# Pairing the sums of the first key tiles and loading block 1's second features in stage one, in a two-layer attention and Mish kernel

## The chip, the cores and the metric

The kernel runs on one core of a Trainium2 chip. A core has a matrix engine (TensorE; PE in the profile, with its weight loads as PEld), a vector engine (VectorE, DVE), an engine for activation functions that also copies (ScalarE, ACT), a general engine (GpSimd, POOL), and a queue engine that issues transfers (SyncE, SP) to 16 DMA engines. Working memory is SBUF; matrix products land in PSUM, in banks. The metric is the device time of one execution in microseconds, and the median of several runs is compared.

## What is computed

A sequence of 2048 rows of 640 numbers goes through attention, dense, attention, dense, each on a layer-normed input and added to it. Attention has 32 heads of 20; its feature map is two softmaxes of a learned projection, one of it and one of its negative.

```python
pq = einsum("bhsd,hdf->bhsf", q, w_phi)          # and pk of k
phi = concatenate([softmax(p), softmax(-p)])     # 40 features for each head
kv = einsum("bhsf,bhsd->bhfd", phi_k, v);  z = phi_k.sum(rows)
o = einsum("bhqf,bhfd->bhqd", phi_q, kv) / (einsum("bhqf,bhf->bhq", phi_q, z) + 1e-6)
x = x + o @ wo
x = x + mish(norm(x) @ w1 + b1) @ w2
```

The key-value sum `kv` needs all rows before the first output row can be made. This splits attention into two stages.

## The kernel before

The 2048 rows are 16 tiles of 128, two to a block, 8 blocks. Products keep float32 precision by splitting both factors into a high and a low part and adding three products (15 matmuls for one half of a projection, 30 for both halves). In the profile the high and low parts of the normed, turned rows are `xth` and `xtl`; weights are `r1h`, `r1l` (keys and values) and `r2h`, `r2l` (queries).

**Stage one** (`attend_first`) runs over the blocks, and in a block over six steps, for instance k0, k1, v0, v1, q0, q1: a projection of keys, values or queries of tile 0 or 1 of the block. Each step is a Python generator. `keys` projects, makes the features in four further pieces (reduce, subtract, exponential, normalise) into a tile `e` of the tag `big` (five buffers) and at last adds the tile to the key-value sum `kva`: 32 small matmuls at L491, one for each head, recorded as 64. `values` evacuates the value rows with a column of ones into a tile `v` (two buffers). `queries` makes features likewise and stores them, transposed, in `e_d[b]` in DRAM with four stores a tile (L508). After each step `advance()` takes all pending generators one piece on, newest first, so the number of `yield`s in a generator sets how many steps later its matmuls come. In the first layer the rows of the next block are turned by TensorE transposes (L334, in `Transposed.turn`) in the last three steps of a block, by `nxt.step()`; in the second layer they come turned from DRAM, and GpSimd writes the low parts (L351). Within stage one the order on the engines is made at compile time by a scheduler that takes what it believes ready, earlier code first; it is not strictly the order of the code.

In block 7's fourth step, the features of block 0 (`load(0)`: two `big` tiles and a small one of the tag `ol`) and the first part of block 1's (`load_groups(1, 0)`, `load_end(1)`) are loaded, and the first two blocks of x are fetched.

**Stage two** (`attend_second`) has its order on TensorE and SP written out by hand. `finish_kv` copies and transposes the sum; `rest` is the last query tile (15), which fills waits; `average(b, t)` multiplies a tile's query features with the sum (L768) and divides. `load(b)` fetches a block's query features. The second part of block 1's features (`load_groups(1, 5)`, a `big` tile) is loaded here, between the two pieces of `finish_kv`, and `load(2)` after the averages of block 0. Query tiles 13 and 15 use the same buffer for their features.

The lines that matter here: L414 (projections), L491 (key-value sums), L334 (transposes), L351 (low parts), L503 (the transpose of query tile 13 on VectorE), L505 (those of the others), L508 (query stores), L720 and L725 (feature loads, large and small), L735 (transposes of the sum), L768 (averages), L135 (every ordered ScalarE copy).

Of the kernel before, what the change touches and what calls it, by code (L numbers as in the profile page):

```python
# [44 lines left out]
def kernel(  # L45
# [45 lines left out]
    for _ in range(30):  # L91
# [22 lines left out]
    x1_d = dram.tile([S, D], F32, name="x1_d")  # L114
    x2_d = dram.tile([S, D], F32, name="x2_d")

    last_act, in_written, last_low, last_load, last_recip, last_fold, last_product, last_sub = (
        [None], [False], [None], [None], [None], [None], [None], [None])

    @contextmanager  # L120
    def written():
# [7 lines left out]
    def act(*args, **kw):  # L129

        if last_act[0] is None or in_written[0]:
            ins = nc.scalar.activation(*args, **kw)
        else:
            with tc.issue_after(last_act[0]):
                ins = nc.scalar.activation(*args, **kw)  # L135
# [324 lines left out]
    def attend_first(layer, x_src, first):  # L460
# [8 lines left out]
            return xt  # L469

        pending = []

        def advance():
            for g in pending[::-1]:
# [5 lines left out]
        def keys(xts, i, v):  # L480
            e = big_tile()
            yield from features(project(xts, i % BT, kv_ws, 0, w=QC), e, False,
                                nc.vector if i == NT - 1 else nc.gpsimd)
            yield
            if i % BT == 0 and BT < i < NT - BT:
                yield
            for r in range(9):
                for j in range(4):
                    h = 3 * (4 * (r // 3) + j) + r % 3
                    if h < H:  # L490
                        nc.tensor.matmul(kva[32 * j:32 * j + DH + 1, 40 * r:40 * r + 40],  # L491
                                         v[:, (DH + 1) * h:(DH + 1) * (h + 1)], e[:, 40 * h:40 * h + 40],
                                         start=(i == 0 and r == 0), stop=(i == NT - 1), skip_group_check=True)

        def queries(xts, i, ps=None):
            e = query_tile(i)
            yield from features(project(xts, i % BT, q_ws, 0, w=QC) if ps is None else ps, e, True)

            b, t = divmod(i, BT)
            if i == NT - BT - 1:  # L500
                yield
                with tc.issue_after(last_recip[0]):
                    nc.vector.transpose(e, e)  # L503
            else:
                nc.vector.transpose(e, e)  # L505
            dst = e_d[b].rearrange("(j f) (t q s) -> t q f j s", f=32, t=BT, s=32)
            for q in range(4):
                nc.sync.dma_start(dst[t, q], e[32 * q:32 * q + 32].rearrange("f (j s) -> f j s", s=32))  # L508
                if b == NB - 1:
                    yield  # L510

        def values(xts, i, v):
            vv = v.rearrange("p (h d) -> p h d", d=DH + 1)
            act(vv[:, :, DH], ident[:, :H], AF.Copy, scale=0.0, bias=1.0)
            if i < BT:
                pv = project(xts, i, kv_ws, D, [one_tile(), one_tile()])
                for c in range(2):
                    act(vv[:, c * H // 2:(c + 1) * H // 2, :DH],
                        pv[c][:, :HC].rearrange("p (h d) -> p h d", d=DH), AF.Copy)
            else:  # L520
                pv = project(xts, i % BT, kv_ws, D)
                act(vv[:, :, :DH].rearrange("p (c h) d -> p c h d", c=2),
                    both(pv).rearrange("p c (h d) -> p c h d", d=DH), AF.Copy)
            yield

# [100 lines left out]
        for b in range(NB):  # L626
# [15 lines left out]
            for n, (kind, t) in enumerate(order):  # L642
# [63 lines left out]
                yield  # L706
                advance()

        return kva, o_ws, loaded, begun, xs, rest()

    def load(b):

        return load_groups(b, 0) + load_groups(b, 5) + load_end(b)

    def load_groups(b, g0):

        t = big_tile()
        src = e_d[b][120 * g0:120 * (g0 + 4) + P]
        src = bass.AP(tensor=src.tensor, offset=src.offset, ap=[[BLK, P], [120 * BLK, 5], [1, BLK]])
        nc.sync.dma_start(t.rearrange("f (g s) -> f g s", s=BLK), src)  # L720
        return [t[:, g * BLK:(g + 1) * BLK] for g in range(5)]

    def load_end(b):
        t = pair_tile(F32)
# [17 lines left out]
        yield  # L742

    def attend_second(x_src, x_dst, acc, fetches, makes, fetch_next, begin_next):
        kva, o_ws, loaded, begun, xs, rest = acc
        rows = {}
        div = [None]

# [57 lines left out]
        with tc.manual_schedule(engines={mybir.EngineType.PE, mybir.EngineType.SP}):  # L806
            kv = finish_kv(kva)
            next(rest)
            next(kv)
            loaded[1] = begun[0] + load_groups(1, 5) + begun[1]  # L810
            next(kv)
            next(rest)
            average(0, 0)
            average(0, 1)
            next(rest)
            loaded[2] = load(2)
            fetches[0]()
            average(1, 0)
            cur = Transposed(rows.pop(0)).all()
# [297 lines left out]
```

## Time and profile before

| | us |
|---|---|
| median of three runs (1356.41, 1356.49, 1360.51) | 1356.49 |
| the profiled execution | 1357.15 |
| its span | 1355.4 |
| stage one, first layer | about 36 to 246 |
| stage two, first layer | about 246 to 345 |
| dense, first layer | about 345 to 700 |
| stage one, second layer | about 700 to 907 |
| stage two, second layer | about 907 to 1006 |
| dense, second layer | about 1006 to 1355 |

How to read the rows that follow. A timeline row has its start and duration in us, the engine, the line, the operation, the output and the input, the shapes and a count of merged instructions; in square brackets stands the idle time before it and what ended it. A row of waits is: who waited, for whom, then the total in us, how often, and the longest. A group row gives count, total busy time, mean in ns, idle time before, and who ended most of it. Matmuls overlap in the pipeline, so their start times, and not their durations, tell what they cost. SPq is SP's queue: a row of it is the issue of a transfer, not the transfer.

### The profile page before, as it was taken

How to read it: one execution, taken by the hardware profiler on the slowest of the kernel's cores; microseconds unless marked ns; L12 is line 12 of the kernel's file. 1: busy time of each engine (PE TensorE's matmuls, PEld its weight loads, DVE VectorE, ACT ScalarE, POOL GpSimd, SP SyncE). 2: the span in 40 equal slices, each digit the busy share in tenths (PEclk: the TensorE clock that was granted, in tenths of full speed). 3: DMA queues.
4: the chain of work that ended last, by engine and by line, in shares of the span. 5: the costliest groups of instructions: out<-in, count | busy, mean ns of one | idle time of the engine just before them, and what ended most of it. 6: DMA issues, size and time to landing. Idle time of an engine off the chain costs nothing.

```text
span 1355.4 us, 30982 instructions
## 1 busy us (share of the span) xinstructions
PE 1347.9 (99%) x12896; PEld 1337.4 (99%) x12896; DVE 1061.2 (78%) x1799; ACT 575.7 (42%) x968; POOL 462.4 (34%) x417
## 2 busy tenths in 40 slices
PE   9999999999999999999999999999999999999999
PEld 9999999999999999999999999999999999999998
DVE  6888988886787887778769788788768776676775
ACT  5444444212454545445443334332236444444443
POOL 3355544334222222222225655634251211111112
PEclk9999999999999999999999999999999999999999
DMA  9544444698714442244474534548974221233200
GB/s 332 166 101 92 95 111 99 173 289 280 216 35 95 117 118 71 61 104 104 140 231 100 122 79 90 95 102 263 282 259 127 79 68 41 88 98 98 70 29 20
DMA packets 352629, 174.11 MB, mean 128 GB/s; under 512 B 287449, under 2 KB 324041, under 8 KB 352489
## 3 DMA queue, kind: packets, MB, share of 16 engines
q1 hardware_dynamic: 352489, 172.14, 46.9%
q8 instruction: 101, 1.65, 0.5%
q14 instruction: 39, 0.32, 0.1%
HBM read 106.23 MB, written 65.86 MB: 127 GB/s over the span
## 4 chain that ended last, share of the span: by engine, by line
PE 94%; DVE 2%; DMA 2%; POOL 1%; SPq 1%; ACT 0%; issue 0%; POOLq 0%; ACTq 0%
PE mm L414 26%; PE one L892 25%; PE mm L943 24%; PE one L414 12%; PE mm L768 2%; PE one L334 2%; PE one L491 1%; PE one L943 1%; DMA xt<-in_x 1%; PE one L768 1%; DVE r L448 1%; DMA raw<-in_wqk_t 0%; DVE m L439 0%; DMA v<-in_wv 0%; DVE r L442 0%; SPq L508 0%
## 5 line engine op out<-in xcount | busy, mean ns | idle before, releaser
L943 PE MATMUL mm<-r2h,ol 128*128 128x320 f32 x1240 | 296.1, 309 | 0.0
L918 POOL TENSOR_TENSOR ol<-big,ol 128x512 fp32r<-128x512 f32 (+1 forms) x98 | 131.1, 1338 | 477.7 <-ACT ol L917 419.5
L892 PE MATMUL one<-xtl,r1h 128*128 128x256 f32 x960 | 268.2, 279 | 0.0
L892 PE MATMUL one<-xth,r1l 128*128 128x256 f32 x960 | 268.0, 279 | 0.0
L892 PE MATMUL one<-xth,r1h 128*128 128x256 f32 x960 | 265.9, 279 | 0.0
L943 PEld LDWEIGHTS mm<-r2h,ol 128*128 128x128 f32 x1240 | 212.5, 188 | 0.0
L943 PE MATMUL mm<-r2l,ol 128*128 128x320 f32 x620 | 191.2, 309 | 0.0
L414 PE MATMUL mm<-r1h,xth 128*128 128x304 f32 (+1 forms) x600 | 185.2, 309 | 0.0
L414 PE MATMUL mm<-r1l,xth 128*128 128x304 f32 (+1 forms) x600 | 183.7, 306 | 0.0
L414 PE MATMUL mm<-r1h,xtl 128*128 128x304 f32 (+1 forms) x600 | 183.6, 306 | 0.2 <-POOL xtl L351 0.2
L892 PEld LDWEIGHTS one<-xtl,r1h 128*128 128x128 f32 x960 | 180.4, 188 | 0.0
L892 PEld LDWEIGHTS one<-xth,r1l 128*128 128x128 f32 x960 | 180.4, 188 | 0.0
L892 PEld LDWEIGHTS one<-xth,r1h 128*128 128x128 f32 x960 | 179.6, 188 | 0.0
L907 DVE TENSOR_SCALAR big<-big 128x512 f32<-128x512 f32 (+1 forms) x98 | 57.2, 583 | 110.0 <-ACT big L905 109.8
L909 ACT ACTIVATE big<-big,two 128x512 f32<-128x512 f32 (+1 forms) x98 | 70.1, 715 | 116.1 <-DVE big L908 116.1
L917 ACT ACTIVATE ol<-big 128x512 fp32r<-128x512 f32 (+1 forms) x98 | 60.9, 622 | 137.6 <-DVE big L916 137.4
L905 ACT ACTIVATE big<-one,b1s 128x256 f32<-128x256 f32 x192 | 80.9, 468 | 89.0 <-PE one L892 88.5
L450 POOL TENSOR_TENSOR r<-r,r 128x1280 f32<-128x1280 f32 x32 | 77.2, 2413 | 118.9 <-DVE r L449 100.8
L943 PEld LDWEIGHTS mm<-r2l,ol 128*128 128x128 f32 x620 | 116.4, 188 | 0.0
L414 PEld LDWEIGHTS mm<-r1h,xth 128*128 128x128 f32 x600 | 112.8, 188 | 0.9
L414 PEld LDWEIGHTS mm<-r1h,xtl 128*128 128x128 f32 x600 | 112.8, 188 | 0.4 <-POOL xtl L351 0.4
L414 PEld LDWEIGHTS mm<-r1l,xth 128*128 128x128 f32 x600 | 112.8, 188 | 0.1
(161 smaller groups left out, 3142.7 us busy)
## 6 DMA issues: line engine op xcount, KB each, us to landing
e_d<-r SPq DMA_DIRECT2D x128, 160.0 KB, 4.2
big<-e_d SPq DMA_DIRECT2D x32, 640.0 KB, 8.0
x_d<-xt SPq DMA_DIRECT2D x23, 640.0 KB, 4.8
xt<-x_d SPq DMA_DIRECT2D x22, 640.0 KB, 5.3
n_d<-xn SPq DMA_DIRECT2D x168, 80.0 KB, 2.3
xt<-in_x SPq DMA_DIRECT2D x16, 640.0 KB, 4.4
xn<-x_d SPq DMA_DIRECT2D x28, 320.0 KB, 4.4
v<-n_d SPq DMA_DIRECT2D x30, 256.0 KB, 3.0
```

What stands on the lines that cost most here:

```text
L334: nc.tensor.transpose(ps[:, c, t * P:(t + 1) * P], self.rows[t][:, (c0 + c) * P:(c0 + c + 1) * P], ident)
L414: last_product[0] = nc.tensor.matmul(ps[:, :w], a[:, sl], r, start=(k == 0 and n == 0), stop=(k == KD - 1 and n == 2)).ins
L448: nc.vector.tensor_reduce(r, eg, axis=AX.X, op=ALU.add)
L450: ins = scale.tensor_tensor(eg, eg, r.unsqueeze(2).to_broadcast([P, 2 * H, DH]), op=ALU.mult).ins
L768: nc.tensor.matmul(po[c][64 * q:64 * q + 64, GW * j:GW * j + w], phs[g][:n, s0:s0 + 64], kvb[:n, g, :w], start=True, stop=True)
L892: nc.tensor.matmul(ph[:, j, :], l, r, start=(n == 0), stop=(n == 3 * KD - 1))
L905: exps[0] = nc.scalar.activation(part(ta, 0)[:, j - js.start], ph[:, j, :], AF.Exp, bias=b1s[:, 2 * pr + j:2 * pr + j + 1]).ins
L907: nc.vector.tensor_scalar_min(e, e, E_CAP)
L909: nc.scalar.activation(r, n, AF.Ln, bias=two)
L917: nc.scalar.activation(ah[:, js], n, AF.Copy)
L918: nc.gpsimd.tensor_tensor(al[:, js], n, ah[:, js].bitcast(F32), op=ALU.subtract)
L943: ins = nc.tensor.matmul(pys[t][c][:, :HC], (ah, ah, al)[n][:, j, t * P:(t + 1) * P], w, start=(f == 0 and n == 0), stop=(f == KF - 1 and ...
```

## The change

- `held(i)` sets how many steps the key-value sum of tile i is held: in the first layer 2 and 0 for block 0, 3 and 1 for block 1, 3 and 2 for blocks 2 to 5, 1 and 0 for block 6, none for block 7; in the second layer 1 and 0 for all blocks but the last. Before it was 1 and 0 for blocks 2 to 6 in both layers, and 0 for blocks 0, 1 and 7. Two tiles of a block so come in the same step, the newer first, and the first group to come opens the accumulation.
- `v_halves`: in even blocks of the first layer the value tiles are two half tiles of the tag `ol` (six buffers, otherwise unused then) in place of `v`; the ones and the values are then written half by half.
- In block 7's fourth step all of block 1's features are loaded: the first part as before, the rest by `load_rest(1)` into three `ol` tiles with four DMAs. `load_groups(1, 5)` in stage two and the separate small load go.
- `load(2)` comes ahead of the second piece of `finish_kv`, and on SP behind the last query store issued so far (`last_store`).

```diff
+        def held(i):
+            b, t = divmod(i, BT)
+            if layer or b == NB - 2:
+                return int(t == 0 and b < NB - 1)
+            return {0: (2, 0), 1: (3, 1), NB - 1: (0, 0)}.get(b, (3, 2))[t]
...
-            if i % BT == 0 and BT < i < NT - BT:
+            for _ in range(held(i)):
                 yield
+            opens = not summed[0]
+            summed[0] = True
...
-                                         v[:, (DH + 1) * h:(DH + 1) * (h + 1)], e[:, 40 * h:40 * h + 40],
-                                         start=(i == 0 and r == 0), stop=(i == NT - 1), skip_group_check=True)
+                                         v[1][c][:, (DH + 1) * g:(DH + 1) * (g + 1)], e[:, 40 * h:40 * h + 40],
+                                         start=(opens and r == 0), stop=(i == NT - 1), skip_group_check=True)
...
+    def v_halves(apart):
+        if apart:
+            return None, [pair_tile(F32).rearrange("p a s -> p (a s)")[:, :VW // 2] for _ in range(2)]
+        v = v_tile()
+        return v, [v[:, :VW // 2], v[:, VW // 2:]]
...
-            vs = [v_tile() for _ in range(BT)]
+            vs = [v_halves(not layer and b % 2 == 0) for _ in range(BT)]
...
-                    begun = load_groups(1, 0), load_end(1)
+                    loaded[1] = load_groups(1, 0) + load_rest(1)
...
+    def load_rest(b):
+        out = []
+        for g0 in (5, 7, 9):
+            t = pair_tile(F32)
+            n = min(2, 10 - g0)
+            src = e_d[b][120 * g0:120 * (g0 + n - 1) + P]
+            src = bass.AP(tensor=src.tensor, offset=src.offset, ap=[[BLK, P], [120 * BLK, n], [1, BLK]])
+            nc.sync.dma_start(t[:, :n], src)
+            out += [t[:, 0], t[:, 1]]
+        nc.sync.dma_start(t[:80, 1], e_d[b][1200:])
+        return out
...
             next(rest)
+            with tc.issue_after(last_store[0]):
+                loaded[2] = load(2)
             next(kv)
-            loaded[1] = begun[0] + load_groups(1, 5) + begun[1]
             next(kv)
             next(rest)
             average(0, 0)
             average(0, 1)
             next(rest)
-            loaded[2] = load(2)
             fetches[0]()
```

The values' evacuation, for a tile held in halves:

```diff
+            for w in [v[0]] if v[0] is not None else v[1]:
+                ones = w.rearrange("p (h d) -> p h d", d=DH + 1)[:, :, DH]
+                act(ones, ident[:, :ones.shape[1]], AF.Copy, scale=0.0, bias=1.0)
+            if v[0] is None or i < BT:
                 for c in range(2):
-                    act(vv[:, c * H // 2:(c + 1) * H // 2, :DH],
+                    act(v[1][c].rearrange("p (h d) -> p h d", d=DH + 1)[:, :, :DH],
                         pv[c][:, :HC].rearrange("p (h d) -> p h d", d=DH), AF.Copy)
```

More of the change, by code (lines that the diff above doesn't have):

```diff
@@ L471, in attend_first @@
         pending = []
+        summed = [False]
+        def held(i):
[3 more added lines that the diff above has]
+            return {0: (2, 0), 1: (3, 1), NB - 1: (0, 0)}.get(b, (3, 2))[t]
         def advance():
@@ L512, in values @@
         def values(xts, i, v):
[L513 to L516, printed above, removed]
+            for w in [v[0]] if v[0] is not None else v[1]:
+                ones = w.rearrange("p (h d) -> p h d", d=DH + 1)[:, :, DH]
+                act(ones, ident[:, :ones.shape[1]], AF.Copy, scale=0.0, bias=1.0)
+            pv = project(xts, i % BT, kv_ws, D, [one_tile(), one_tile()] if i < BT else None)
+            if v[0] is None or i < BT:
                 for c in range(2):
-                    act(vv[:, c * H // 2:(c + 1) * H // 2, :DH],
+                    act(v[1][c].rearrange("p (h d) -> p h d", d=DH + 1)[:, :, :DH],
                         pv[c][:, :HC].rearrange("p (h d) -> p h d", d=DH), AF.Copy)
             else:
-                pv = project(xts, i % BT, kv_ws, D)
-                act(vv[:, :, :DH].rearrange("p (c h) d -> p c h d", c=2),
+                act(v[0].rearrange("p (c h d) -> p c h d", c=2, d=DH + 1)[:, :, :, :DH],
                     both(pv).rearrange("p c (h d) -> p c h d", d=DH), AF.Copy)
@@ L707, in rest @@
                 advance()
-        return kva, o_ws, loaded, begun, xs, rest()
+        return kva, o_ws, loaded, xs, rest()
     def load(b):
@@ L744, in attend_second @@
     def attend_second(x_src, x_dst, acc, fetches, makes, fetch_next, begin_next):
-        kva, o_ws, loaded, begun, xs, rest = acc
+        kva, o_ws, loaded, xs, rest = acc
         rows = {}
```

8 lines of the change are left out of this document (5 added, 3 removed).

## The prediction

> **What bounds the kernel now.** I read the page first, then TensorE's waits, then the chain of waits, then the timeline of TensorE around every key-value sum (L491) and around the two places where it stands idle.
>
> ```profile
> span 1355.4 us, 30982 instructions
> PE   1347.9 (99%) x12896; PEld 1337.4 (99%) x12896; DVE 1061.2 (78%) x1799; ACT 575.7 (42%) x968; POOL 462.4 (34%) x417
> ```
> ```profile
> PE 94%; DVE 2%; DMA 2%; POOL 1%; SPq 1%; ACT 0%; issue 0%; POOLq 0%; ACTq 0%
> ```
> ```profile
> PE one L334 <- ACT r L135: 1.8, 2, 1.3
> ```
> ```profile
> PEld one L491 <- issue: 3.4, 19, 0.2
> ```
>
> TensorE is the bound (94% of the chain) and is fed nearly always. The change multiplies the same matrices in the same shapes, so it can win only three things: the 1.8 us in which the transposes of L334 wait for ScalarE, twice (once per layer); the cost of entering and leaving a sum, which shows as 0.18 us (3.4 / 19) of weight-load idle at each group; and waits on late operands. It can lose only by new waits.
>
> The execution profiled took 1357.15 us, its span of 1355.4 and 1.75 around it; the median of the three runs shown is 1356.49. I work out a difference in the profiled execution and take it off the median. 0.3% (4.07 us) is about what a measurement of this kernel can tell from no change.
>
> **Part 1: what a pair saves.** A single sum between projections, a pair, a single ahead of four transposes, and four transposes alone, each from the last matmul before it to the second after it (the first one after starts slow):
>
> ```profile
> 78.55 0.30 PE L414 MATMUL mm<-r1h,xtl 128*128 128x304 f32 x1
> 78.78 0.83 PE L491 MATMUL one<-big,v 128*21 128x40 f32 x64
> ...
> 79.79 0.30 PE L414 MATMUL mm<-r1l,xth 128*128 128x304 f32 x1
> 79.93 0.30 PE L414 MATMUL mm<-r1h,xtl 128*128 128x304 f32 x1
> ```
> ```profile
> 110.93 0.30 PE L414 MATMUL mm<-r1h,xtl 128*128 128x304 f32 x1
> 111.17 1.48 PE L491 MATMUL one<-big,v 128*21 128x40 f32 x128
> ...
> 112.81 0.30 PE L414 MATMUL mm<-r1l,xth 128*128 128x304 f32 x1
> ```
> ```profile
> 62.22 0.30 PE L414 MATMUL mm<-r1h,xtl 128*128 128x304 f32 x1
> 62.45 0.83 PE L491 MATMUL one<-big,v 128*21 128x40 f32 x64
> 63.21 0.65 PE L334 MATMUL one<-ident,xn 128*128 128x128 f32 x4
> ...
> 63.85 0.31 PE L414 MATMUL mm<-r1l,xth 128*128 128x320 f32 x1
> ```
> ```profile
> 92.83 0.31 PE L414 MATMUL mm<-r1h,xtl 128*128 128x320 f32 x1
> 92.98 0.60 PE L334 MATMUL one<-ident,xn 128*128 128x128 f32 x4
> ...
> 93.56 0.31 PE L414 MATMUL mm<-r1l,xth 128*128 128x320 f32 x1
> ```
>
> Matmuls start 0.14 us apart (79.79 to 79.93), so two steps, 0.28 to 0.29 us, come off each stretch. A single costs 1.24 - 0.28 = 0.96 us, a pair 1.88 - 0.28 = 1.60: **one pair instead of two singles saves 0.32 us.** A single with transposes behind it costs 1.63 - 0.28 = 1.35, the transposes alone 0.73 - 0.29 = 0.44: the single is 0.91 there, so **standing ahead of transposes saves 0.05.**
>
> The Trainium skill (TensorEngine Tiling (Array Packing), Key Properties) says that a change of the tiling mode drains TensorE; the sums use 32-column tiles and the transposes the whole array, so by it the neighbourhood saves no drain, and the trace agrees with its 0.05 us. If instead a neighbour saved a whole entry and exit (0.32 us), the six pairs moved there would give 1.9 us, not 0.3.
>
> First layer, tiles 0 to 3: now 2 x 0.91 + 2 x 0.96 (tiles 0 and 1 already stand ahead of transposes) = 3.74; after, two pairs ahead of transposes, 2 x 1.55 = 3.10; saves 0.64. Blocks 2 to 5 are pairs already and move two steps on, to transposes: 4 x 0.05 = 0.2. Second layer: four singles become two pairs, 0.64. Together 1.5 us of pure TensorE time.
>
> **Part 2: what a later sum uncovers.** The singles of tile 2 stand, in both layers, ahead of (or inside) the first projection of block 2 and cover the wait for its operand; the change moves them behind it. With the 0.32 of the first pair, TensorE comes to that operand 0.96 + 0.32 = 1.28 us sooner. In the first layer (VectorE writes the operand, TensorE uses it):
>
> ```profile
> 81.68 0.41 DVE L351 TENSOR_TENSOR xtl<-one,xth 128x256 fp32r<-128x256 f32 x1
> ```
> ```profile
> 81.05 0.30 PE L414 MATMUL mm<-r1l,xth 128*128 128x304 f32 x1
> 81.19 0.30 PE L414 MATMUL mm<-r1h,xth 128*128 128x304 f32 x1
> ...
> 82.73 0.44 PE L414 MATMUL mm<-r1h,xtl 128*128 128x304 f32 x2
> ```
>
> It is ready at 82.09 and used at 82.73: 0.64 us of slack, and the compiler's schedule has already put the second half's matmuls (from 81.19) ahead of the ones that need it. Bounds for this layer's 0.64: all of it, if the schedule fills again, or nothing, if 1.28 - 0.64 = 0.64 is waited. I take 0.6, as this very place shows the filling. In the second layer GpSimd writes it and is late already:
>
> ```profile
> 746.72 0.74 POOL L351 TENSOR_TENSOR xtl<-xn,xth 128x256 fp32r<-128x256 f32 x1
> ```
> ```profile
> 744.36 0.83 PE L491 MATMUL one<-big,v 128*21 128x40 f32 x64
> ...
> 747.05 0.30 PE L414 MATMUL mm<-r1l,xth 128*128 128x304 f32 x1
> 747.51 0.41 PE L414 MATMUL mm<-r1h,xtl 128*128 128x304 f32 x1 [0.15 <-POOL xtl L351]
> ...
> 749.94 0.83 PE L491 MATMUL one<-big,v 128*21 128x40 f32 x64
> ```
>
> Here the step from 747.05 to 747.51 holds 0.32 us of waiting. If the order of the matmuls stays as it is, TensorE still goes on at 747.5 whatever was saved before, and behind it stands a pair (1.60) instead of the single at 749.94 (0.96): a **loss of 0.64**. If the schedule fills the wait with the other half or the pair, it gains 0.64 + 0.32 = 0.96. The rows show filling once (81.19) and none once (747.05); I take a gain of 0.3 and keep -0.96 and +0.64 as ends.
>
> **Part 3: the start of stage two.** First layer:
>
> ```profile
> 243.30 1.50 DVE L503 STREAM_TRANSPOSE r<-r 128x1280 f32<-128x1280 f32 x1
> ```
> ```profile
> 236.05 3.34 SPq L508 DMA_DIRECT2D e_d<-r  x4
> 245.27 0.38 SPq L720 DMA_DIRECT2D big<-e_d  x1
> 245.75 7.23 SPq L508 DMA_DIRECT2D e_d<-r  x4
> ```
> ```profile
> 243.31 0.16 POOL L430 MEMSET r<- 128x32 f32 x1 [1.28 <-DMA e_d<-r]
> ```
> ```profile
> 255.44 0.74 ACT L135 ACTIVATE r<-one 128x304 f32<-128x304 f32 x2 [5.16 <-DMA e_d<-r]
> ```
> ```profile
> 255.92 0.44 PE L334 MATMUL one<-ident,xn 128*128 128x128 f32 x2 [1.28 <-ACT r L135]
> ```
>
> Query tile 13 is transposed by 244.80, but its four stores stand on SP behind block 1's second features (L720 at 245.27, which waits for the last sums to free its buffer) and share the DMA engines with it: 7.23 us to issue against 3.34 for tile 12's. They land at 255.4; only then may ScalarE write tile 15 into the same buffer, free its two PSUM banks, and let the transposes go on: 1.28 us idle. The change takes that load out (block 1's rest comes in stage one, in three small tiles and four DMAs for the former two) and puts load(2) behind the stores by issue_after. Tile 12's stores took 243.3 - 236.05 = 7.2 us from first issue to last landing; from 244.85 that is 252.1, when TensorE still has work to 254.6 (255.92 - 1.28). So the **1.28 us goes.** What is late next is the split of these rows for the first projection of stage two; ScalarE and VectorE do it right behind the transposes, so it comes 1.28 sooner too. The second layer's wait has the same cause:
>
> ```profile
> 916.49 0.44 PE L334 MATMUL one<-ident,xn 128*128 128x128 f32 x2 [0.53 <-ACT r L135]
> ```
>
> 0.53 goes with it: **1.81 us in all**. Bounds: 0, if the stores stay late, and 1.81; I take 1.8, the room being 254.6 - 252.1 = 2.5 us. load(2), three DMAs, now waits on SP for the last sums too, but behind the stores; behind it wait only the first weight fetch and load(3), and its data are used by block 2's averages, after the whole projection of block 0. Its two big buffers are those of the last key tiles, so load(3) takes load(0)'s, no later than now. The four DMAs of stage one stand where SP already waits for sums.
>
> **ScalarE.** Even blocks of the first layer evacuate their values into two half tiles:
>
> ```profile
> L135 ACT ACTIVATE v<-mm 128x640 f32<-128x640 f32 x28 | 19.8, 707 | 50.1 <-PE mm L414 50.1
> L135 ACT ACTIVATE v<-ident 128x32 f32<-128x32 f32 x32 | 8.2, 258 | 0.0
> L135 ACT ACTIVATE v<-one 128x320 f32<-128x320 f32 x8 | 3.3, 434 | 5.2 <-PE one L414 5.2
> ```
>
> 2 x 0.434 - 0.707 = 0.16, and 0.26 for a second column of ones: 0.42 us for each of six tiles, 0.26 for the two of block 0, 3.0 us in all, hidden by the idle that the first row has ahead of it (50.1 us over 28). Its price without cover is those 3.0 us.
>
> **Sum:** 1.8 + 0.6 + 0.2 + 0.3 = 2.9 us off. 1357.15 becomes 1354.25 in a profiled execution, and **1353.6** against the median.
>
> **Rivals.** *All of it arrives*: 1.81 + 0.64 + 0.2 + 0.96 = 3.6, 1352.9. For it: the scheduler filled at 81.19. Against it: at 747.05 it did not see GpSimd late. *Only the boundary pays*, because the later sums uncover the waits of part 2, or because the schedule slips the sums apart again (as at 78.78, inside a projection): 1.8 + 0 + 0.2 - 0.64 = 1.4, 1355.1. *Slower: SP is blocked in stage one.* Its small tiles are the ones that now hold block 6's values, free only when tiles 12 and 13 are summed:
>
> ```profile
> SPq L720 <- PE one L491: 9.7, 2, 8.3
> ```
>
> Today SP waits up to 8.3 us there with nothing urgent behind. If the four new loads are put ahead of four query stores, these are 8.3 us late, ScalarE cannot evacuate the next query tile, and TensorE, with one projection (4.2 us, 30 x 0.14) of spare bank, loses 4.1 us a layer; from 4.2 us of lateness on it costs. Both layers: 8.2 - 2.9 = 5.3 slower, 1361.8; one: 1357.7. Against it: a load is placed only when its tile is free.
>
> **From this to the numbers.** Forecast 0.50, all of it 0.20, only the boundary 0.18, slower 0.12. The first three lie within 0.3% (1352.4 to 1360.6); a sum of 3.6 comes over 4.07 only with half a microsecond of scatter (1357.15 against 1356.49), for which I give 0.13 out of these three. Of the slower case, 0.08 is over 0.3%. Same 0.79. The range is from the full gain with that scatter, 1352.1, to one blocked layer, 1357.7.
>
> **What would show it.** TensorE's waits of L334 on ScalarE gone; the L491 groups, ten in a layer, become eight pairs, each near 1.48 us, and the weight loads' idle there near 16 x 0.18 = 2.9; the stores of tile 13 issued within 3.5 us of 244.9; the wait for GpSimd near 747 tells layer two's sign. Wrong would be: idle of L414 on L351 of over 1 us, stores of tile 13 still behind a load, or SP waits on L491 with L508 behind them.

## The result and the profile after

The changed kernel takes 1359.85 us (median of 19 runs, 1356.89 to 1365.95), the kernel before beside it 1356.83 (19 runs, 1355.73 to 1360.96): a ratio of 1.0019, 95% interval [1.001, 1.0028]. It is slower by 0.2%, where 0.2% less was forecast. The execution profiled took 1358.03 us, with a span of 1356.3, 0.9 over the span before. The page of the changed kernel (L421, L509, L341, L358, L326, L456 and L457 are the former L414, L491, L334, L351, L319, L449 and L450) and its waits of TensorE:

```profile
span 1356.3 us, 31003 instructions
...
PE 81%; DVE 8%; POOL 1%; DMA 1%; issue 0%; SPq 0%; ACT 0%; DVEq 0%; POOLq 0%; ACTq 0%
```
```profile
PE mm L421 <- DVE xtl L358: 2.3, 3, 1.1
PE one L509 <- POOL big L457: 1.2, 1, 1.2
PE mm L421 <- POOL xtl L358: 0.4, 1, 0.4
```

VectorE now holds 8% of the chain, where it held 2%. The two waits of L334 on ScalarE are gone from the list, and new ones stand in it: three for VectorE's third low part (xtl, 128x256) and, in the second layer, one of a sum for GpSimd (1.2 us); the projection's wait for GpSimd's low part was there before and has grown from 0.2 to 0.4 us. Where they fall is seen by comparing a fixed event of each stage, the third transposes made for the next block, in TensorE's timeline of the kernel before and then of the changed one:

```profile
102.45 0.38 PE L334 MATMUL one<-ident,xn 128*128 128x128 f32 x2
...
130.75 0.38 PE L334 MATMUL one<-ident,xn 128*128 128x128 f32 x2
...
159.04 0.38 PE L334 MATMUL one<-ident,xn 128*128 128x128 f32 x2
...
187.32 0.38 PE L334 MATMUL one<-ident,xn 128*128 128x128 f32 x2
```
```profile
102.11 0.38 PE L341 MATMUL one<-ident,xn 128*128 128x128 f32 x2
...
109.26 0.41 PE L421 MATMUL mm<-r1h,xtl 128*128 128x304 f32 x1 [0.61 <-DVE xtl L358]
...
131.22 0.38 PE L341 MATMUL one<-ident,xn 128*128 128x128 f32 x2
...
138.82 0.41 PE L421 MATMUL mm<-r1h,xtl 128*128 128x304 f32 x1 [1.07 <-DVE xtl L358]
...
160.78 0.38 PE L341 MATMUL one<-ident,xn 128*128 128x128 f32 x2
...
167.95 0.41 PE L421 MATMUL mm<-r1h,xtl 128*128 128x304 f32 x1 [0.64 <-DVE xtl L358]
...
189.91 0.38 PE L341 MATMUL one<-ident,xn 128*128 128x128 f32 x2
```

At 102 the changed kernel is 0.34 us ahead; one block later it is 0.47 behind, then 1.74, then 2.59. Each of the three steps between the rows has one wait, at the first projection of blocks 3, 4 and 5, and is longer by that wait and 0.2 us more. Stage one of layer one loses 2.93 us there (87.80 against 84.87).

Stage two wins. Its beginning in the first layer, in TensorE's timeline before and then after (the transposes of the sums, the ten transposes of the averages, the first averages behind them):

```profile
246.72 0.49 PE L735 MATMUL one<-ident,xn 128*120 128x128 f32 x3
...
253.55 1.09 PE L334 MATMUL one<-ident,xn 128*128 128x128 f32 x8
...
256.29 1.38 PE L768 MATMUL mm<-kvb,big 120*64 120x63 f32 x40
```
```profile
249.23 0.49 PE L767 MATMUL one<-ident,xn 128*120 128x128 f32 x3
...
256.05 1.31 PE L341 MATMUL one<-ident,xn 128*128 128x128 f32 x10
257.29 0.80 PE L800 MATMUL mm<-kvb,big 120*64 120x63 f32 x20
```

From the first row to the last it was 9.57 us and is 8.06. The ten transposes stand in one group with no idle; from their start to the averages it is 1.24 us where it was 2.74, of which 1.28 was the wait. To the start of the dense part the whole stage gains 1.52 us, in the second layer 1.07. Stage one of the second layer, from its first key projection to the transposes of the sums, goes from 207.75 us (699.97 to 907.72) to 208.82 (700.98 to 909.80). Together: 0.23 from a later start (stage one's first transposes at 36.23 against 36.00), -0.57 up to the rows at 102, +2.93, -1.52, +1.07, -1.07, and -0.07 in what is left is 1.0 us at the last matmul, about the 0.9 of the spans.

**Why the low part is late.** VectorE and GpSimd of the kernel before, ahead of block 4's first projection (VectorE's rows first):

```profile
133.34 0.68 DVE L351 TENSOR_TENSOR xtl<-one,xth 128x512 fp32r<-128x512 f32 x1
...
135.39 0.41 DVE L351 TENSOR_TENSOR xtl<-one,xth 128x256 fp32r<-128x256 f32 x1
135.72 0.54 DVE L449 RECIPROCAL r<-r 128x64 f32<-128x64 f32 x1
136.18 0.16 DVE L319 SCALAR_TENSOR_TENSOR stats<-mv,stats 128x1 f32<-128x1 f32 x2
```
```profile
136.34 2.97 POOL L450 TENSOR_TENSOR big<-big,r 128x1280 f32<-128x1280 f32 x1 [0.24 <-DVE stats L319]
```

And of the changed kernel:

```profile
133.63 0.68 DVE L358 TENSOR_TENSOR xtl<-one,xth 128x512 fp32r<-128x512 f32 x1
134.23 0.54 DVE L456 RECIPROCAL r<-r 128x64 f32<-128x64 f32 x1
134.69 1.48 DVE L446 TENSOR_REDUCE m<-r 128x32 f32<-128x640 f32 x2
136.09 2.34 DVE L326 SCALAR_TENSOR_TENSOR stats<-mv,stats 128x1 f32<-128x1 f32 x2
138.35 0.41 DVE L358 TENSOR_TENSOR xtl<-one,xth 128x256 fp32r<-128x256 f32 x1
```
```profile
132.32 2.37 POOL L457 TENSOR_TENSOR big<-big,r 128x1280 f32<-128x1280 f32 x1
134.78 0.46 POOL L323 TENSOR_SCALAR ve<-mv 128x1 f32<-128x1 f32 x2
135.33 0.70 POOL L324 TENSOR_TENSOR stats<-ve,neg_half 128x2 f32<-128x2 f32 x1
135.99 2.36 POOL L457 TENSOR_TENSOR big<-big,r 128x1280 f32<-128x1280 f32 x1
```

The second low part (128x512) starts at nearly the same time in both (133.34 and 133.63), and the third, whose high part ScalarE had written by 133.13, starts 3 us later, at 138.35 against 135.39. Two things make this up. The reciprocal and the next block's layer norm statistics now stand ahead of it; and the statistics, which took 0.16 us, take 2.34, as long as GpSimd's multiplication runs beside them. The edit moved the sums on TensorE, but the order of VectorE and GpSimd is made by the same scheduler at compile time, and here it has turned round. At block 3 the statistics stood ahead of the low part in the kernel before too, but early (0.17 us at 102.92); now they come at 105.04, behind one multiplication of GpSimd, and take 2.38 us beside the next.

### The profile page after: what moved, and what is told of

Read it like the earlier page. It is cut to its first block, busy times and chain, and to the rows that moved or that the text cites. A ratio compares the mean times of both kernels' runs of the same rounds, so it can differ in the third digit from the quotient of the medians.

```text
span 1356.3 us, 31003 instructions
## 1 busy us (share of the span) xinstructions
PE 1346.3 (99%) x12896; PEld 1336.2 (99%) x12896; DVE 1066.0 (79%) x1799; ACT 577.3 (43%) x982; POOL 462.7 (34%) x417
## 4 chain that ended last, share of the span: by engine, by line
PE 81%; DVE 8%; POOL 1%; DMA 1%; issue 0%; SPq 0%; ACT 0%; DVEq 0%; POOLq 0%; ACTq 0%
PE one L924 25%; PE mm L975 24%; PE mm L421 17%; PE one L421 10%; PE mm L800 2%; DVE r L455 2%; DVE m L446 1%; PE one L341 1%; PE one L509 1%; DVE r L523 1%; DVE xn L813 1%; PE one L975 1%; DVE r L449 1%; DVE xtl L358 1%; DMA e_d<-r 1%; DVE r L456 0%
## 5 line engine op out<-in xcount | busy, mean ns | idle before, releaser
L421 PE MATMUL mm<-r1h,xtl 128*128 128x304 f32 (+1 forms) x600 | 183.7, 307 | 2.7 <-DVE xtl L358 2.3
L421 PE MATMUL mm<-r1h,xth 128*128 128x304 f32 (+1 forms) x600 | 184.7, 308 | 0.0
L421 PE MATMUL mm<-r1l,xth 128*128 128x304 f32 (+1 forms) x600 | 183.6, 306 | 0.0
L457 POOL TENSOR_TENSOR r<-r,r 128x1280 f32<-128x1280 f32 x32 | 78.6, 2458 | 113.1 <-DVE r L456 104.3
L421 PEld LDWEIGHTS mm<-r1h,xtl 128*128 128x128 f32 x600 | 112.8, 188 | 3.6 <-DVE xtl L358 3.1
L421 PEld LDWEIGHTS mm<-r1h,xth 128*128 128x128 f32 x600 | 112.8, 188 | 0.5
L421 PEld LDWEIGHTS mm<-r1l,xth 128*128 128x128 f32 x600 | 112.8, 188 | 0.1
```

The source lines that it names most:

```text
L421: last_product[0] = nc.tensor.matmul(ps[:, :w], a[:, sl], r, start=(k == 0 and n == 0), stop=(k == KD - 1 and n == 2)).ins
L457: ins = scale.tensor_tensor(eg, eg, r.unsqueeze(2).to_broadcast([P, 2 * H, DH]), op=ALU.mult).ins
```

## The experiments

The table gives for each kernel the three steps between third transposes (as in the rows above; 28.3 before), stage one of the second layer, and the median against the kernel before that ran beside it.

| kernel | three steps of stage one, layer one | stage one, layer two | median | ratio [95%] |
|---|---|---|---|---|
| before | 28.30, 28.29, 28.28 | 207.75 | 1356.83 | |
| changed | 29.11, 29.56, 29.13 | 208.82 | 1359.85 | 1.0019 [1.001, 1.0028] |
| e0_again | 32.40, 28.45, 29.91 | 210.45 | 1360.27 | 1.0025 [1.0016, 1.0035] |
| e1_held_back | 29.68, 28.28, 28.29 | 208.96 | 1358.40 | 1.0006 [0.9997, 1.0015] |
| e2_boundary | 28.30, 28.29, 28.28 | 207.77 | 1354.56 | 0.9981 [0.9972, 0.999] |
| e5_stats_behind | 28.23, 28.22, 28.23 | 208.91 | 1356.11 | 0.9996 [0.9986, 1.0005] |
| e6_best | 28.27, 28.29, 28.28 | 207.68 | 1353.48 | 0.9969 [0.9958, 0.998] |
| e7_moved_alone | 28.25, 33.67, 28.23 | 208.12 | 1360.37 | 1.0019 [1.001, 1.0028] |
| e9_layer2_first | 31.77, 28.32, 29.81 | 208.22 | 1359.88 | 1.0018 [1.001, 1.0027] |
| e10_layer2_later | 28.28, 28.28, 28.28 | 210.66 | 1355.71 | 0.9989 [0.9981, 0.9997] |
| e11_memset_behind | 28.28, 28.28, 28.28 | 207.18 | 1353.32 | 0.997 [0.9958, 0.9982] |
| e12_layer2_whole | 28.28, 28.29, 28.28 | 207.78 | 1354.38 | 0.9983 [0.9973, 0.9992] |

**e0_again**: the changed kernel, unedited.

> The changed kernel once more, for a second profile of it. Theory (VectorE's order): in stage one of layer one each first projection of blocks 3, 4 and 5 waits for the third low part (xtl of 128x256), because the two small statistics instructions stand ahead of it on VectorE and last about as long as GpSimd's multiplication of the second key tile (2.36 us). The first profile had 0.61, 1.07 and 0.64 us of it and lost 2.85 us between the third transposes of block 2's stage and those of block 5's. This run shows the same three waits, 2 to 4 us in all; the median time is 2.5 to 3.5 us over the kernel before. Rival (chance of one execution): the waits stand at other places, or the loss between these two points is under 1 us.

The waits are there, but not the same three. The profile of this execution lists

```profile
PE mm L421 <- DVE xtl L358: 3.8, 2, 2.4
```

and the first of them, with VectorE's statistics of x and low part ahead of it, and the granted clock (the number behind the count in brackets) in stretches of 1 us behind it:

```profile
98.34 1.28 DVE L314 BATCH_NORM_STATS2 bn<-xt 128x6 f32<-128x320 f32 x3 [4.02 <-DMA xt<-in_x]
...
110.09 0.41 DVE L358 TENSOR_TENSOR xtl<-one,xth 128x256 fp32r<-128x256 f32 x1
```
```profile
111.00:112.00 1.00, 1.00 (x6) 0.53 0.78 305
112.00:113.00 1.00, 1.00 (x6) 0.50 0.07 23
113.00:114.00 1.00, 1.00 (x6) 0.50 0.83 323
114.00:115.00 1.00, 1.00 (x8) 0.77 0.02 5
```

VectorE's whole list hangs here on the load of x, which came 1.3 us later than in the first profile (98.34 against 97.05), and TensorE was 0.47 us earlier (101.64 against 102.11): the wait grew by these two, from 0.61 to 2.4 us. Behind it TensorE ran at about half its clock, which costs 0.47 + 0.50 + 0.50 + 0.23 = 1.7 us more: together the 4.1 us by which the first step is longer than before. Block 4, behind this long loss, pays almost nothing (28.45), though VectorE's list has the same order and its statistics take 2.38 us there too: TensorE comes to the low part no earlier than VectorE has it. In the second layer the clock falls to half once more, for about 1.7 us of its 210.45. So the loss differs between executions, and the one profiled first was a mild one: 1358.03 against a median of 1359.85.

**e1_held_back**: the pairs of blocks 2 to 5 of layer one stand where they stood before; all else is the change.

```diff
-            return {0: (2, 0), 1: (3, 1), NB - 1: (0, 0)}.get(b, (3, 2))[t]
+            return {0: (2, 0), 1: (3, 1), NB - 1: (0, 0)}.get(b, (1, 0))[t]
```

> The changed kernel, with the sums of blocks 2 to 5 of layer one put where the kernel before had them (the pair between the two key projections); the first four key tiles stay in pairs, the half tiles of v and the rest of the change too. VectorE's instruction list then has the third low part ahead of the statistics for blocks 4 and 5, and still behind them for block 3. Theory (moving the pairs of blocks 2 to 5 turned VectorE's order round): the waits of 1.07 and 0.64 us at the first projections of blocks 4 and 5 are gone, the one at block 3 (0.61 us) stays; the span is 1.9 to 2.1 us below the changed kernel's, about 1.1 to 1.3 us below the span before (1355.4). Rival (the half tiles of v with their doubled evacuations, or the pairs of blocks 0 and 1, are what delays the low parts): all three waits stay, and the time is within 0.5 us of the changed kernel's.

As the theory has it: the steps of blocks 4 and 5 are 28.28 and 28.29 again, the one with block 3 keeps its wait (1.1 us), and its span is 1354.7, 1.6 below the changed kernel's where 1.9 to 2.1 was expected, as the wait that stays is longer than the 0.61. The half tiles of v are in this kernel, so they aren't the cause at blocks 4 and 5: these two waits come from the moved pairs of blocks 2 to 5. Block 3's wait stays, so it comes with the pairs of blocks 0 and 1 (or with block 0's half tiles, which no run has without them). In the median this kernel is still 1.6 us over the one before; the profiled execution (1356.52) was the fastest of 11, so the others lost more than these rows show.

**e5_stats_behind**: the sums stay as changed, and only the statistics of the next block's layer norm, from the reading of x on, are held behind the low part.

```diff
-            with (tc.issue_after((last_fold if b == 3 else last_sub)[0]) if b in (1, 3) else nullcontext()):
+            with (tc.issue_after((last_fold if b == 3 else last_sub)[0]) if b in (1, 3) else tc.issue_after(last_low[0]) if b > 3 else nullcontext()):
```

> The changed kernel with one thing more: the layer norm's statistics of blocks 4 to 7 of layer one (GpSimd's and VectorE's small instructions) may be issued only behind the third low part of the block ahead. All sums stay where the change put them. VectorE's instruction list then has the third low part ahead of the statistics in every block. Theory (it is the order on VectorE that costs the time, not the new place of the sums on TensorE): the three waits at the first projections of blocks 3 to 5 are gone, and stage one of layer one runs 2.7 to 3.0 us shorter than the changed kernel's, so that the span is some 2 us under the one before (1355.4). Rival (the low part is late for want of its inputs, or GpSimd's multiplication holds VectorE up whatever stands next in its list): the low part itself takes 2 us or more where the statistics did, the waits stay, and the time is within 0.5 us of the changed kernel's.

All three waits go, and the steps are 28.23, 28.22 and 28.23, from

```profile
102.30 0.38 PE L341 MATMUL one<-ident,xn 128*128 128x128 f32 x2
...
186.98 0.38 PE L341 MATMUL one<-ident,xn 128*128 128x128 f32 x2
```

This is shown, then: the order on VectorE and GpSimd costs the time, not the new place of the sums. The rival is answered too: the low part takes 0.41 us as ever, also with GpSimd at work beside it (at 133.76). The edit takes the wait for x's load from ahead of the low part together with the slow statistics, so what each is worth by itself is not separated. With the waits gone the new place even saves 0.06 us a block against 28.29. Of the three steps' 3.1 us, 0.6 is given back at the end of the stage (31.70 us from the last block's third transposes to those of the sums, against 31.11; a sum waits 0.4 us there for a multiplication), which was not followed further; the span is 1354.3, 2.0 below the changed kernel's.

**e2_boundary**: of the change only the loads at the end of stage one and the place of load(2). All sums and v tiles are as in the kernel before; the edit against the changed kernel:

```diff
             if layer or b == NB - 2:
-                return int(t == 0 and b < NB - 1)
-            return {0: (2, 0), 1: (3, 1), NB - 1: (0, 0)}.get(b, (3, 2))[t]
+                return int(t == 0 and (not layer or b > 1) and b < NB - 1)
+            return int(t == 0 and 1 < b < NB - 1)
...
-            vs = [v_halves(not layer and b % 2 == 0) for _ in range(BT)]
+            vs = [v_halves(False) for _ in range(BT)]
```

> The kernel before with one part of the change alone: block 1's second features loaded in stage one in small tiles, and block 2's load moved ahead of the last key sums. All sums stand where the kernel before has them; v is in one tile. Theory (the boundary is worth what the traces show of it, 1.52 us in layer one and 1.07 in layer two, and costs stage one nothing): 2.6 us under the kernel before, ratio 0.9981; the third transposes of stage one come at the same times as before (within 0.1 us), the ten transposes before the averages run without a gap in both layers. Rival one (part of the gain belongs to the earlier sums): 1.8 us or less. Rival two (the small loads hold SP up and delay stores and features in stage one): under 0.5 us, with later transposes in the last block of stage one.

Every stage time came out: no change in stage one of either layer, 105.62 and 105.63 us from the transposes of the sums to the dense part, the same as in the changed kernel, and 2.25 us off the median (1354.56 against 1356.81; 2.6 was expected). The rival with SP held up is dead. The span of the execution profiled (1355.9) says nothing here: TensorE ran at half its clock from about 33.4 to 40.3 us, behind two waits of 0.84 and 0.38 us and ahead of everything that was edited, which costs 3.4 us.

**e7_moved_alone**: e2 with the move of blocks 2 to 5 and nothing else.

```diff
-            return int(t == 0 and 1 < b < NB - 1)
+            if layer or not 2 <= b <= 5:
+                return int(t == 0 and 1 < b < NB - 1)
+            return (3, 2)[t]
...
-            vs = [v_halves(False) for _ in range(BT)]
+            vs = [v_halves(not layer and b in (2, 4)) for _ in range(BT)]
```

> The boundary part, and of the sums only the move of the pairs of blocks 2 to 5 behind the next projections and transposes (half tiles of v in blocks 2 and 4); the first four key tiles of both layers singly as before. VectorE's instruction list has the statistics ahead of the third low part for blocks 3, 4 and 5, as in the changed kernel. Theory (this move alone turns the order round and costs the time): waits at the first projections of blocks 4 and 5, most likely at block 3 too, and stage one of layer one 2 to 3 us longer than with the boundary part alone (its three block steps of 28.3 us become 29 to 30), median 0 to 1 us over the kernel before. Rival (the waits need the first four pairs, which bring TensorE to the low part earlier): block steps of 28.3 us, 2.6 us under the kernel before.

The cost is there without the first pairs: 1360.37 against e2's 1354.56, but not in the shape expected. There is one wait, not two or three:

```profile
141.02 0.62 PE L421 MATMUL mm<-r1h,xtl 128*128 128x304 f32 x1 [3.30 <-DVE xtl L358]
```

of 3.3 us, with half the clock for 3.4 us behind it (33.67 us for that step). Blocks 3 and 5 pay nothing although VectorE's list has the statistics ahead of the low part there too. The rows of this kernel at block 3, and then at block 5, show why:

```profile
102.44 0.22 DVE L326 SCALAR_TENSOR_TENSOR stats<-mv,stats 128x1 f32<-128x1 f32 x2
...
106.83 0.41 DVE L358 TENSOR_TENSOR xtl<-one,xth 128x256 fp32r<-128x256 f32 x1
```
```profile
167.48 2.38 DVE L326 SCALAR_TENSOR_TENSOR stats<-mv,stats 128x1 f32<-128x1 f32 x2
169.79 0.41 DVE L358 TENSOR_TENSOR xtl<-one,xth 128x256 fp32r<-128x256 f32 x1
```

At block 3 the statistics meet no multiplication and take 0.22 us. At block 5 they are as slow as at block 4, but TensorE, 5.4 us later after block 4's step, needs the low part only when it is there. The order of VectorE alone is therefore not enough. What makes the low part late is the statistics standing ahead of it, behind one multiplication of GpSimd and beside the next; whether TensorE waits for it depends on how early TensorE itself comes. The 0.37 us by which this kernel's second layer is longer is a wait for ScalarE (0.37 us at 782) that no other list has.

**e9_layer2_first**: the changed kernel with the second layer's block 1 summed singly.

```diff
-                return int(t == 0 and b < NB - 1)
+                return int(t == 0 and (not layer or b != 1) and b < NB - 1)
```

> The changed kernel, with layer two's block 1 summed singly as before; its block 0 stays a pair. Layer two's stage one (from its first key projection to the averages) took 207.75 us before and 208.82 to 208.96 with both pairs. Theory (the loss comes from the pair of block 1: TensorE runs ahead of GpSimd's third low part and its multiplication, and the pair's first ten matmuls stand where they wait 1.21 us for GpSimd): 207.4 to 207.8 us, the wait of 1.21 us is gone, and the time is some 1.1 to 1.4 us below the changed kernel's. Rival (the pair of block 0 puts GpSimd's instructions in another order, and its third low part comes late by itself): 208.4 us or more, with a wait for the low part of 1 us or more.

Between the two: 208.22, so of the 1.07 us lost 0.6 went with block 1's pair, and 0.47 stayed with block 0's. GpSimd and then TensorE of this kernel:

```profile
743.74 0.16 POOL L437 MEMSET r<- 128x32 f32 x1 [1.87 <-DMA e_d<-r]
743.82 2.37 POOL L457 TENSOR_TENSOR big<-big,r 128x1280 f32<-128x1280 f32 x1
...
749.71 0.72 POOL L358 TENSOR_TENSOR xtl<-xn,xth 128x256 fp32r<-128x256 f32 x1
```
```profile
750.49 0.41 PE L421 MATMUL mm<-r1h,xtl 128*128 128x304 f32 x1 [0.97 <-POOL xtl L358]
```

The memset of a query tile has moved ahead of a key tile's multiplication in GpSimd's list (the kernel before has it behind), and stands there 1.87 us waiting for stores; all behind it, the low part last, comes later (the low part 47.28 us from the stage's first projection, 46.75 in the kernel before). The rival named the right kind of cause.

**e10_layer2_later**: e6 with both pairs in the second layer, block 1's one step later.

```diff
-                return int(t == 0 and (not layer or b > 1) and b < NB - 1)
+                return int(t == 0 and b < NB - 1) if not layer or b != 1 else (2, 1)[t]
```

> The kernel of e6_best, with layer two's first four key tiles in pairs, block 0's as in the change, block 1's one step later, behind the first value projection of block 2. Theory (what costs in layer two is TensorE waiting for GpSimd ahead of block 2's first projection, and no sum is left to fill it): a wait for the low part of 1.0 to 1.7 us at that projection, layer two's stage one at 208.2 to 208.8 us, 0.5 to 1.0 us over the kernel before's 207.75. Rival (it was the split pair and its own wait that cost, and the two pairs save their 0.64 us as the prediction has it): 207.1 us.

Of the place of the pair it tells little: the schedule put its first ten records into block 2's first projection all the same, where they wait 1.21 us for GpSimd. This time TensorE's clock was at half speed behind it (from about 745.9 to 749.3), so that 208.9 became 210.66. In the medians against the kernel before, the two pairs of the second layer cost 2.2 us here (1.3 under it, where e6 is 3.55 under it).

**e6_best**: e2, with layer one's first pairs, and the statistics of block 4 behind block 3's low part.

```diff
-            with (tc.issue_after((last_fold if b == 3 else last_sub)[0]) if b in (1, 3) else nullcontext()):
+            with (tc.issue_after((last_fold if b == 3 else last_sub)[0]) if b in (1, 3) else tc.issue_after(last_low[0]) if b == 4 else nullcontext()):
...
-            return int(t == 0 and 1 < b < NB - 1)
+            return {0: (2, 0), 1: (3, 1), NB - 1: (0, 0)}.get(b, (1, 0))[t]
...
-            vs = [v_halves(False) for _ in range(BT)]
+            vs = [v_halves(not layer and b % 2 == 0) for _ in range(BT)]
```

> The boundary part and layer one's first four key tiles in pairs (half tiles of v in blocks 0, 2, 4 and 6 as in the change); blocks 2 to 5 summed where the kernel before has them, layer two's first four sums single as before, and the statistics of block 4 issued behind the third low part of block 3. Theory: each block of layer one's stage one takes 28.3 us between its transposes and the next block's, as before; the first pairs save 0.58 us ahead of that, the boundaries 1.52 and 1.07, layer two's stage one costs what it did before (207.75 us from its first key projection to the averages): 3.2 us under the kernel before, span near 1352.2, ratio 0.9977. Rival (the half tiles of v, or the first pairs, cost stage one something that shows only when the waits are gone): 2.0 us or less under the kernel before.

3.55 us under the kernel before (3.2 was expected), and no new wait in stage one. Every term stands: steps of 28.3, 207.68 in the second layer, both starts of stage two at their new length.

**e11_memset_behind**: e6 with the second layer's block 0 as a pair, and GpSimd's memset for one query tile held in its old place (scales lists GpSimd's multiplications).

```diff
-                return int(t == 0 and (not layer or b > 1) and b < NB - 1)
+                return int(t == 0 and (not layer or b != 1) and b < NB - 1)
...
-        nc.gpsimd.memset(eh[:, 1, :, DL:], 0.0)
+        with (tc.issue_after(behind) if behind is not None else nullcontext()):
+            nc.gpsimd.memset(eh[:, 1, :, DL:], 0.0)
...
+                                behind=scales[-1] if layer and i == 2 else None)
```

> The kernel of e6_best with layer two's block 0 as a pair (as in e9_layer2_first), and GpSimd's memset of block 1's first query tile issued behind its multiplication of the key tile ahead, the order of the kernel before. In e9 the memset stood ahead of that multiplication and waited 1.87 us for the stores of an earlier query tile, TensorE then waited 1.0 us for the third low part, and layer two's stage one took 208.22 us, against 207.75 before. Theory (that wait on GpSimd is what makes the pair cost): GpSimd does not stand idle there, TensorE's wait for the low part is 0.3 to 0.6 us, the stage takes 207.6 to 207.9 us. Rival (the order of GpSimd's list is no cause; the multiplication itself comes as late): the wait of 1.0 us and the 208.2 us stay.

207.18 us, 0.57 less than before and 1.04 less than e9. GpSimd's rows:

```profile
737.58 2.38 POOL L460 TENSOR_TENSOR big<-big,r 128x1280 f32<-128x1280 f32 x1 [0.80 <-DVE r L459]
739.89 0.16 POOL L440 MEMSET r<- 128x32 f32 x1
...
743.54 0.75 POOL L358 TENSOR_TENSOR xtl<-xn,xth 128x256 fp32r<-128x256 f32 x1
```

The memset no longer waits, the low part comes 46.18 us from the stage's first projection, and TensorE has no wait for it left. So the place of one memset of 0.16 us was what made block 0's pair cost. At 1353.32 us this is the best version; against e6's 1353.48 the runs don't tell it apart.

**e12_layer2_whole**: e11, with block 1 of the second layer as a pair too, the pair held whole behind block 2's first key projection.

```diff
-                return int(t == 0 and (not layer or b != 1) and b < NB - 1)
+                return int(t == 0 and b < NB - 1)
...
+            with (tc.issue_after(last_product[0]) if layer and i in (2, 3) else nullcontext()):
...
```

> As e11_memset_behind, and block 1's sums of layer two as a pair too, held whole behind the first key projection of block 2 (in e10 its first ten records stood inside that projection all the same). This is the case of the prediction's upper bound: the two pairs save 0.64 us, and TensorE comes 1.28 us sooner to the third low part, with nothing to do there. Theory: a wait of 1.3 to 1.7 us for the low part, stage one of layer two 208.2 to 208.5 us. Rival (the two pairs save their 0.64 us, the split pair was the trouble): 207.1 us. A clock at half speed behind the wait, as in e10, would come on top and is left out of the stage's time.

207.78 us with a wait of 0.84: neither the theory's 208.2 nor the rival's 207.1. Against e11, which keeps block 1's single sum where it was, it is 0.6 slower: the prediction's 0.32 for a pair, less the wait of 0.84 that the single sum had filled, is a loss of 0.52. Why the wait is less than the 1.3 expected was not tested; GpSimd's low part came earlier than was reckoned in e11 too.

## Why the prediction was wrong

- **Blocks 2 to 5 "move two steps on, to transposes: 4 x 0.05 = 0.2".** This is the step that failed. The price on TensorE was right (0.06 a block in e5). Left out was that the moves change the order in which VectorE and GpSimd do their work, and so when the low parts of blocks 3 to 5 come. Of the 2.93 us lost in the profile, the steps with blocks 4 and 5 (2.1 us) go with these moves and the one with block 3 (0.8) with the first pairs: e1 keeps only the latter, e7 has none at block 3. Measured against the kernel before beside each, the moves alone cost 5.6 us in the median (e7 3.3 over it, e2 2.25 under it). The wait that comes with the first pairs costs some 3 us, estimated in the same way: e1, which has it, is 5.1 over e6, which doesn't, and 2.2 of these are the second layer's by e10. The two don't add up, because a block behind a long loss pays little. The prediction's list of signs had the wait ("idle of L414 on L351"), but slack was worked out at block 2 alone, and from the order of before. What turned the scheduler's order was not looked into.
- **Part 2, second layer: a gain of 0.3, between 0.96 and -0.64.** It was a loss of 1.07, outside both ends, for the same fault: the ends were made with GpSimd's rows of before. Instead a memset came to stand ahead and GpSimd itself was later (e9, e11), and the ten records that fill the projection wait for GpSimd too (1.21 us). With GpSimd's order mended, both pairs come out even (e12, 207.78 against 207.75), inside the range; pairing block 0 alone gains 0.50 over e6, the 0.32 of a pair and the 0.17 of a wait for the low part that goes.
- **Part 1 and the first layer's half of part 2: 0.64, with 0.6 taken.** Right: 0.57 up to the third transposes of block 2's stage (66.45 to 65.88 us from the first transposes), and no wait at block 2's first projection. The sums are eight groups in layer one (in layer two one of the eight is split), and the weight loads' idle at them is 3.0 us over 16, where 2.9 was expected.
- **Part 3: 1.8 us.** Right in its mechanism and too small: 2.59. The two waits (1.28 and 0.53) go. Besides, each layer's ten transposes are no longer split in two groups, which costs 0.22 us each time (2.74 - 1.28 and 1.99 - 0.53 are 1.46, against 1.24 now), and the second layer's averages lose a hitch of 0.33. Tile 13's stores now go out ahead of the loads (the row of eight holds tile 12's four and tile 13's four):

```profile
238.88 12.67 SPq L526 DMA_DIRECT2D e_d<-r  x8
251.66 1.88 SPq L739 DMA_DIRECT2D big<-e_d  x2
```

Tile 13's take from 247.69, right behind its transpose, to 251.55 to issue: 3.9 us, where 3.5 was forecast and 7.23 measured before. ScalarE may write at 254.44, 6.8 us after the first of them (7.2 forecast, 9.7 before).

- **ScalarE's 3.0 us are hidden.** Right: blocks with half tiles take 28.28 us in e1 and e6, as before.
- **The rivals.** No rival had the loss of the first layer. "Only the boundary pays" came nearest: it had a loss in the second layer (0.64, measured 1.07). The slower one, SP blocked in stage one, did not happen (e2). The difference lies within 0.3%, as was held likeliest, but on the other side, and the time above the range's end of 1357.7. (The range's lower end, 1352.9 less the scatter of 0.66, is 1352.2 and not 1352.1.)

## What to carry to other kernels

A pair, or any group, moved on the engine that bounds the kernel can also move what the compiler orders around it: after such an edit compare the instruction lists of the other engines, and look at what now stands ahead of the one small operand that the bounding engine needs next. A late operand can be mended by pinning the few small instructions ahead of it (statistics in e5, a memset in e11), which keeps the move; where the move is worth as little as here (0.06 us a block), giving it back (e6) does as well. And price a stall's own size as an uncertain one: the same program waited 0.6 us in one execution and 2.4 in the next.

## What the runs showed of the hardware

Two statistics instructions of 128x1 on VectorE take 0.16 to 0.22 us with GpSimd idle and 2.3 us with a 128x1280 multiplication of GpSimd beside them (1.29 beside a 128x640 subtraction of 1.28, in e5): they end when it does. The Trainium skill (GPSIMD Engine Reference, the table of its specification) says that GpSimd shares its SBUF interfaces with VectorE and that instructions with two SBUF inputs contend; these are such, and the trace agrees with it; how long it lasts the rows tell.

TensorE's granted clock falls to 0.50 for about 3.4 us behind some of the short waits: behind 2.4 us (e0), 1.75 (e9), 3.3 (e7) and the 1.21 with 0.36 of the second layer in e10 and e0, but not behind the same 1.21 with 0.36 in the changed kernel's own profile, e1 and e5, nor behind e0's 1.42, e9's 1.32 or e1's 1.1. In e2 it stayed at 0.50 for twice as long, 6.9 us, behind waits of 0.84 and 0.38. Each stretch of 3.4 us costs 1.7 us, and comes on top of the wait. The Trainium skill (TensorE: Matmul & The Clock Gate, What's actually happening) has the clock halved after at least one idle window of about 3.4 us that runs free of the kernel. The length of the slow stretch and its coming and going agree with such a window, but waits of 1.2 us (e2's two together) to 3.3 us were enough here, so here the measurement differs from a window that is wholly idle. What part of a window has to be idle stays open; it was not tried.
